# Third slot's weights in the second buffer, the inverse over two shares fewer, and one 64-column product for V and X from the ninth chunk

## The chip, the cores and the metric

The kernel runs on one core of one Trainium2 chip. A core has TensorE (PE in the rows, its weight loads apart as PEld), VectorE (DVE), ScalarE (ACT), GpSimd (POOL) and SyncE (SP, which here only issues transfers). The metric is the device time of one execution in microseconds, the median of three runs: 1097.17 us (1096.41 to 1097.25).

## The reference

Three parts follow one another. An attention recurrence over 4 batches x 8 heads (32 heads in all), 768 steps, head width 40, in float32:

```
y[t]  = r[t] @ state
Sa    = state @ a[t]
state = state * w[t] - outer(Sa, b[t]) + outer(v[t], k[t])
```

Its output, as 3072 tokens of 320 numbers, goes through a dense layer pair, `h = x @ w_in; x = max(0.01 h, h) @ w_out` (320 to 2048 to 320), and then through a mixture of eight experts of which each token uses one:

```
expert = argmax(x @ w_gate);  gate = softmax(x @ w_gate)[expert]
out    = gate * (relu(x @ w1[expert]) @ w2[expert])      # 320 -> 1024 -> 320
```

## The kernel before

**Attention in chunks.** The 768 steps are cut into 24 chunks of 32. Inside a chunk the recurrence becomes products of small matrices, one set for each head. Head n has its keys in tile `L` (three bands of rows, multiplied by state-side values in `Vx`), its queries in `Rr`, its values in `Vt`. A chunk goes through the steps `s1` to `s6`, most of them in halves a and b: `s1` forms right-hand sides, `s2` multiplies them by the inverse of a triangular matrix (`TT`) to get the corrected values X, `s3` forms the next state, `s3x` turns X around, `s4` multiplies queries by V and by X, `s5` makes the output, `s6` carries the state over. `s4` issues for each of 16 pairs of heads and each of V and X one product of a 40-row, 32-column weight with 32 columns of queries; in float32 each of them appears in the trace as two weight loads and two matmuls, 128 of each kind in a chunk (line 469). The V half of `Vt` comes by `load3` (line 384), the X half is written by ScalarE in `s3x` (line 459).

**Preparation and inverse.** Ahead of that, `prep` makes decays, keys and triangular matrices for a coming chunk, mostly on VectorE and GpSimd. For four chunks at a time GpSimd inverts the triangular matrices (`inverse`, lines 309 and 315, tile `Tinv`): 62 steps of one instruction each, of which VectorE does the first and the last, a transposition that leaves `TT` (line 323). From group to group this is needed by `s2` of chunks 8, 12, 16 and 20.

**The dense pair in halves.** Word `H` in the orders is half a step of the dense pair (`layer1` line 722, `layer2` line 738, with `g`, `gh`, `gl` between them on ScalarE, VectorE and GpSimd). The order of the whole first part is written out by hand as strings of words (`START`, `STEP`, `LATE`, `END`), played by `overlap`: one string a chunk from chunk 5 on. Word `w`, nine times in each such string, is a share of the inverse: it issues the remaining steps divided by the remaining shares, rounded up, so that the last share of a group of four chunks issues the last step.

**The experts in slots.** `Moe2.go` runs sixteen slots of 256 tokens, one expert each. In slot j TensorE does eight rounds f of `layer1` and `layer2` (lines 1152 and 1168); in the same rounds ScalarE and VectorE split the next slot's raw weights into two parts (`split`, lines 1114 to 1124), SP loads raw weights for the slot after (`load`, line 1072, five pieces of 512 or 640 KB), a gather fetches its tokens (`fetch`, lines 1086 to 1096: row numbers `sid` by SP, then rows `xg` by GpSimd), and TensorE turns the next slot's tokens (`xpose`, line 1135). Raw weights lie in `raw`; only slot 3 (`NE - 1`) uses a second tile, `raw2`. The load of slot 2 thus waits until the split of slot 1 has read `raw`, and it and the load of slot 3 behind it are issued piece by piece from round 1 of slot 0 on. Between them in SP's queue stand the row numbers of slot 2 and the last two writes of routed tokens (`x2d`, line 806), which wait for the gather of slot 2.

Of the kernel before, what the change touches and what calls it, by code (L numbers as in the profile page):

```python
# [73 lines left out]
def layouts(r, k, v, w, a, b, moe_w_in, moe_w_out, moe2_w_gate, moe2_w1, moe2_w2):  # L74
# [10 lines left out]

    def words(x):
        x = np.ascontiguousarray(x)
        return x.view(np.int64) if x.dtype == np.float64 else x
# [48 lines left out]
class Attn:  # L137


    def __init__(s, tc, ctx, i, k, xT, bad, psA):  # L140
        s.tc = tc
        nc = s.nc = tc.nc
# [16 lines left out]
        s.Vt = c.tile([128, 2, NU, 32], F32, name="Vt")  # L159
# [221 lines left out]
    def load3(s, c):  # L381
        nc = s.nc
        nc.sync.dma_start(s.Rr[64:104], s.i["hr"][c].rearrange("q (n d) -> q n d", d=32))
        nc.sync.dma_start(s.Vt[64:104, 0], s.i["hvt"][c].rearrange("q (n d) -> q n d", d=32))
        s.lamY = s.p1.tile([128, 16, 33], F32, name="lamY")
        nc.sync.dma_start(s.lamY.rearrange("p a b -> p (a b)"), s.dl[c])
# [631 lines left out]
class Moe2:  # L1018
# [36 lines left out]
    def source(s, j):  # L1055
        return s.raw2 if j == NE - 1 else s.raw
# [127 lines left out]
    def go(s, ready, finish):  # L1184
# [125 lines left out]
def overlap(tc, at, m1, plan):  # L1310
# [70 lines left out]
    def play(order, here=0):  # L1381
# [4 lines left out]
        for word in order:  # L1386
# [97 lines left out]
```

## Time and profile before

| | |
|---|---|
| median of three runs | 1097.17 us |
| the profiled execution, its own time | 1093.98 us |
| its span from first to last instruction | 1092.3 us |
[...]
| PE busy, weight loads busy | 926.7 us (85%), 870.0 us (80%) |
| DVE, ACT, POOL busy | 805.5, 529.9, 492.3 us |
| the chain that ended last, by engine | PE 41%, DVE 26%, DMA 12%, issue 8%, ACT 6%, POOL 5% |

All times in the rows are microseconds from the span's start. The chunks of the attention run until about 762, with the dense pair beside them; the rest of the dense pair ends at about 822, and the expert slots fill the remainder. A busy share says little alone: a wait is read from the bracket at the end of a timeline row, which says how long the engine stood idle before it and what released it. "Issue" as the releaser means that the profile shows nothing that the engine waited for. A window row gives busy time and, in brackets, the number of instructions of each engine that began in a stretch, then the granted clock.

### The profile page before, as it was taken

Reading aid. Unit: us, or ns where it says so; the run is one execution under the profiler, and the core shown is the slowest. Engines: PE = TensorE matmul, PEld = TensorE weight load, DVE = VectorE, ACT = ScalarE, POOL = GpSimd, SP = SyncE. Lnnn points to the kernel's source line nnn. Section 1 sums busy time; section 2 is a strip of 40 time slices with the busy share of each in tenths; the row PEclk is TensorE's granted clock in tenths of the full one; section 3 lists DMA queues with packets and bytes.
Section 4 is the critical chain, followed back from the end, with each engine's and each line's share of the span. In section 5 each row is a group of like instructions: output and inputs, shape, how many; then the busy total and the mean of one; then the engine's idle time right before and its main releaser. Section 6 shows DMA issues by size and latency. Waiting matters only on the chain.

```text
span 1092.3 us, 40673 instructions
## 1 busy us (share of the span) xinstructions
PE 926.7 (85%) x16854; PEld 870.0 (80%) x16854; DVE 805.5 (74%) x1910; ACT 529.9 (49%) x1316; POOL 492.3 (45%) x680
## 2 busy tenths in 40 slices
PE   2266677977799898989979998999999899999994
PEld 1255576867788887878879888998899799999994
DVE  8988778766878686968777766667657777787761
ACT  3545455653435444444435443444456556666651
POOL 5124135214883399446964685333553132332211
PEclk9999997788999899999999998999999999999997
DMA  8978876857546566574655542332425747444530
GB/s 249 228 211 228 231 198 185 214 137 215 137 126 172 143 166 158 129 176 131 172 151 146 128 80 72 92 82 54 152 91 129 219 158 225 126 146 140 161 104 17
DMA packets 143991, 166.04 MB, mean 152 GB/s; under 512 B 67931, under 2 KB 105451, under 8 KB 143671
## 3 DMA queue, kind: packets, MB, share of 16 engines
q1 hardware_dynamic: 133687, 144.20, 48.8%
q10 hardware_dynamic: 5760, 10.49, 3.3%
q0 software_dynamic: 4352, 8.69, 2.5%
q8 instruction: 134, 2.20, 0.9%
q14 instruction: 58, 0.48, 0.2%
HBM read 127.62 MB, written 42.27 MB: 156 GB/s over the span
## 4 chain that ended last, share of the span: by engine, by line
PE 41%; DVE 26%; DMA 12%; issue 8%; ACT 6%; POOL 5%; SPq 1%; POOLq 0%; DVEq 0%; ACTq 0%
PE psH L722 8%; PE psX L738 8%; PE epy L1168 8%; PE psH L1152 6%; DVE junk L762 4%; PE eph L1152 3%; DVE g L727 2%; DMA Pq<-Ms 2%; DVE Rr L472 2%; DMA L<-dKBr 2%; PE psA L414 2%; POOL Tinv L315 2%; DVE lam L226 2%; DMA raw<-hwe 1%; POOL itmp L309 1%
## 5 line engine op out<-in xcount | busy, mean ns | idle before, releaser
L729 POOL TENSOR_TENSOR gl<-g,gh 128x256 fp32r<-128x256 f32 x192 | 157.3, 822 | 216.9 <-ACT gh L728 199.6
L727 DVE TENSOR_TENSOR g<-psH,g 128x256 f32<-128x256 f32 x192 | 81.2, 423 | 103.3 <-ACT g L726 99.8
L728 ACT CAST gh<-g 128x256 fp32r<-128x256 f32 x192 | 77.9, 406 | 161.8 <-DVE g L727 159.6
L738 PE MATMUL psX<-woh,gh 128*128 128x320 f32 x384 | 134.6, 351 | 2.0 <-ACT woh L649 1.1
L738 PE MATMUL psX<-woh,gl 128*128 128x320 f32 x384 | 124.9, 325 | 4.2 <-POOL gl L729 4.0
L726 ACT ACTIVATE g<-psH 128x256 f32<-128x256 f32 x192 | 73.5, 383 | 108.6 <-PE psH L722 83.3
L738 PE MATMUL psX<-wol,gh 128*128 128x320 f32 x384 | 123.7, 322 | 0.0
L762 DVE SCALAR_TENSOR_TENSOR junk<-X,raws 128x320 bf16<-128x320 f32 x160 | 92.9, 581 | 5.5 <-ACT X L759 3.5
L722 PE MATMUL psH<-xh,wih 128*128 128x256 f32 x384 | 87.2, 311 | 3.6 <-DVE g L727 3.5
L309 POOL TENSOR_TENSOR itmp<-Tinv 128x30 f32<-128x30 f32 (+14 forms) x120 | 71.5, 596 | 33.5 <-DVE Tinv L301 26.3
L738 PEld LDWEIGHTS psX<-woh,gl 128*128 128x128 f32 x384 | 76.5, 199 | 7.6 <-POOL gl L729 7.3
L738 PEld LDWEIGHTS psX<-woh,gh 128*128 128x128 f32 x384 | 76.6, 199 | 6.2 <-ACT woh L649 1.3
L722 PE MATMUL psH<-xl,wih 128*128 128x256 f32 x384 | 80.6, 293 | 0.0
L722 PE MATMUL psH<-xh,wil 128*128 128x256 f32 x384 | 80.1, 291 | 0.0
L1180 POOL DMA_INDIRECT out<-ey,sid x32 | 32.5, 1015 | 104.6 <-ACT ey L1179 99.4
L265 PE MATMUL psA<-AtI,KB 40*64 40x72 f32 x1408 | 44.1, 266 | 41.7 <-DVE KB L243 18.4
L315 POOL TENSOR_TENSOR Tinv<-Tinv,itmp 128x30 f32<-128x30 f32 (+14 forms) x120 | 74.3, 619 | 7.8
L738 PEld LDWEIGHTS psX<-wol,gh 128*128 128x128 f32 x384 | 77.2, 201 | 0.4 <-DVE wol L650 0.3
L265 PEld LDWEIGHTS psA<-AtI,KB 40*64 40x64 f32 x1408 | 36.0, 164 | 48.8 <-POOL woh L242 18.4
L722 PEld LDWEIGHTS psH<-xh,wih 128*128 128x128 f32 x384 | 66.4, 201 | 8.6 <-DVE g L727 5.8
L722 PEld LDWEIGHTS psH<-xl,wih 128*128 128x128 f32 x384 | 63.2, 202 | 0.0
L1156 DVE SCALAR_TENSOR_TENSOR ehl<-psH,ehh 128x256 fp32r<-128x256 f32 x86 | 36.1, 420 | 36.4 <-ACT ehh L1155 36.1
(289 smaller groups left out, 2751.3 us busy)
## 6 DMA issues: line engine op xcount, KB each, us to landing
raw<-hwe SPq DMA_DIRECT2D x48, 512.0 KB
raw<-hwe SPq DMA_DIRECT2D x32, 640.0 KB
in<-h SPq DMA_DIRECT2D x23, 521.0 KB
KB<-h SPq DMA_DIRECT2D x22, 512.0 KB
L<-dKBr SPq DMA_DIRECT2D x24, 320.0 KB
dKBr<-KBr SPq DMA_DIRECT2D x22, 320.0 KB
lamY<-dl SPq DMA_DIRECT2D x24, 264.0 KB
dl<-lam SPq DMA_DIRECT2D x22, 264.0 KB
```

Of the source, the lines that this page charges most:

```text
L265: nc.tensor.matmul(box[i][64 * j:64 * j + 64, k, :], z["KB"][o, p, :], z["AtI"][o, p, :], start=True, stop=True)
L309: eng.tensor_tensor(out=box["v"], in0=T[:, k + 1:32, k:k + 1].to_broadcast([128, n, k]), in1=T[:, k:k + 1, 0:k].to_broadcast([128, n, k]), ...
L315: eng.tensor_tensor(out=T[:, k + 1:32, 0:k], in0=T[:, k + 1:32, 0:k], in1=box["v"], op=ALU.add)
L722: nc.tensor.matmul(ps[:, 0:256], w, x, start=(n == 0), stop=(n == 7))
L726: nc.scalar.activation(out=g, in_=ps[:, 0:256], func=AF.Copy, scale=0.01)
L727: nc.vector.tensor_tensor(out=g, in0=ps[:, 0:256], in1=g, op=ALU.max)
L728: nc.scalar.copy(out=gh, in_=g)
L729: return gh, gl, lambda: nc.gpsimd.tensor_tensor(out=gl, in0=g, in1=gh, op=ALU.subtract)
L738: nc.tensor.matmul(s.x2[t][:, 0:DM], x[:, o], w[:, f, :], start=(f == 0 and n == 0), stop=(f == NF - 1 and n == 2))
L762: nc.vector.scalar_tensor_tensor(out=s.junk, in0=X[:, t, 0:DM], scalar=1.0, in1=s.wg[:, e], op0=ALU.mult, op1=ALU.mult, accum_out=lg[:, t, ...
L1152: nc.tensor.matmul(ps, w, x, start=(n == 0), stop=(n == 7))
L1168: nc.tensor.matmul(s.y[t][:, 0:DM], x[:, o], w, start=(f == 0 and n == 0), stop=(f == 7 and n == 2))
```

## The change

There are three edits.

- `source`: slots 0, 1 and 3 use `raw`, slot 2 and all from slot 4 on use `raw2`. The five pieces of slot 2 are issued at once in round 0 of slot 0, those of slot 3 from round 5 of slot 0 on, behind the split of slot 1, which reads the same tile.
- `play`, word `w`: the remaining steps are divided by two shares fewer.
- From chunk 8 (`PAIRED`) on, V and X of a head lie side by side in `Vt`, 64 columns a head. The host lays out V with zeros where X goes, so `load3` moves 320 KB in place of 160 KB and writes the X places too; `s3x` writes X into every second block of 32; `s4` issues one product with a 64-column weight where it issued two.

```
--- before.py
+++ after.py
@@ -62,6 +62,7 @@
     "i H l t H H H H t l l H t l H H H l H s H H H H H H s H H H H H H s H H t H H H t H t H H c s s H H H H s H H l H H H H H H H H s H H H s x s H l H l H "
     "l s l H H "
 )
+PAIRED = 8
 NFIX = NT // SL + E // 2
 NTB = 8 * CAP + 8 * SL
 XW = DM + 64 + 1
@@ -82,6 +83,10 @@
 
     def flat(x):
         return np.ascontiguousarray(x.reshape(B, 2, 4, NC, C, D).transpose(3, 5, 1, 0, 2, 4).reshape(NC, D, NU * C))
+
+    def twice(x):
+        x = x.reshape(NC - PAIRED, D, NU, C)
+        return np.ascontiguousarray(np.concatenate([x, np.zeros_like(x)], axis=3).reshape(NC - PAIRED, D, 2 * NU * C))
 
     def words(x):
         x = np.ascontiguousarray(x)
@@ -101,7 +106,8 @@
         "nr": r, "nk": k, "nv": v, "nw": w, "na": a, "nb": b,
         "h1": np.ascontiguousarray(np.concatenate([hw, pad(pair(a)), pad(np.concatenate([pair(k), pair(b)], axis=-1))], axis=2)),
         "hr": flat(r),
-        "hvt": flat(v),
+        "hvt": np.ascontiguousarray(flat(v)[:PAIRED]),
+        "hvx": twice(flat(v)[PAIRED:]),
         "hv": np.ascontiguousarray(v.reshape(B, 2, 4, NC, C, D).transpose(3, 4, 1, 0, 2, 5).reshape(NC, C, NU * D)),
         "hwi": words(np.concatenate([moe_w_in[0:128], moe_w_in[128:256], np.concatenate([wt[:, 0:FF // 2], wt[:, FF // 2:]], axis=0)], axis=1)),
         "hwo": words(moe_w_out.reshape(NF, 128, DM).transpose(1, 0, 2).reshape(128, NF * DM)),
@@ -156,7 +162,7 @@
         s.L = [c.tile([128, NU, 40], F32, name=f"L{j}") for j in range(2)]
         nc.gpsimd.memset(s.Vx[1][32:64], 0.0)
         s.Rr = c.tile([128, NU, 32], F32, name="Rr")
-        s.Vt = c.tile([128, 2, NU, 32], F32, name="Vt")
+        s.Vt = c.tile([128, 2 * NU * 32], F32, name="Vt")
         s.Xq = c.tile([128, 512], F32, name="Xq")
         nc.vector.memset(s.Xq, 0.0)
         s.Pq = c.tile([128, 32, 32], F32, name="Pq")
@@ -381,7 +387,10 @@
     def load3(s, c):
         nc = s.nc
         nc.sync.dma_start(s.Rr[64:104], s.i["hr"][c].rearrange("q (n d) -> q n d", d=32))
-        nc.sync.dma_start(s.Vt[64:104, 0], s.i["hvt"][c].rearrange("q (n d) -> q n d", d=32))
+        if c < PAIRED:
+            nc.sync.dma_start(s.Vt[64:104, 0:32 * NU], s.i["hvt"][c])
+        else:
+            nc.sync.dma_start(s.Vt[64:104], s.i["hvx"][c - PAIRED])
         s.lamY = s.p1.tile([128, 16, 33], F32, name="lamY")
         nc.sync.dma_start(s.lamY.rearrange("p a b -> p (a b)"), s.dl[c])
 
@@ -451,7 +460,10 @@
 
     def s3x(s, c):
         nc = s.nc
-        vt = s.Vt[64:104, 1].rearrange("d (q g) t -> d g q t", q=4)
+        if c < PAIRED:
+            vt = s.Vt[64:104, 32 * NU:].rearrange("d (q g t) -> d g q t", q=4, t=32)
+        else:
+            vt = s.Vt[64:104].rearrange("d (n w t) -> d n w t", w=2, t=32)[:, :, 1].rearrange("d (q g) t -> d g q t", q=4)
         ps = s.bank()
         for g in range(4):
             nc.tensor.transpose(ps[:, 128 * g:128 * g + 128], s.Xq[:, 128 * g:128 * g + 128], s.k.ident)
@@ -464,9 +476,13 @@
         for p in range(8 * b, 8 * b + 8):
             for i in range(2):
                 n = 16 * i + p
+                if c >= PAIRED:
+                    nc.tensor.matmul(
+                        ps[64 * i:64 * i + 64, 32 * p:32 * p + 32], s.Vt[64:104, 64 * n:64 * n + 64], s.Rr[64:104, n, :], start=True, stop=True)
+                    continue
                 for w in range(2):
-                    o = 64 * i + 32 * w
-                    nc.tensor.matmul(ps[o:o + 32, 32 * p:32 * p + 32], s.Vt[64:104, w, n, :], s.Rr[64:104, n, :], start=True, stop=True)
+                    o, a = 64 * i + 32 * w, 32 * (NU * w + n)
+                    nc.tensor.matmul(ps[o:o + 32, 32 * p:32 * p + 32], s.Vt[64:104, a:a + 32], s.Rr[64:104, n, :], start=True, stop=True)
         o = slice(8 * b, 8 * b + 8)
         for i in range(2):
             nc.vector.tensor_tensor(
@@ -1053,7 +1069,7 @@
         s.nh = 0
 
     def source(s, j):
-        return s.raw2 if j == NE - 1 else s.raw
+        return s.raw if j < 2 or j == NE - 1 else s.raw2
 
     def load(s, j):
 
@@ -1206,10 +1222,13 @@
                 if sp and f % 3 != 2:
                     sp.pop(0)()
                 step(PACE[min(j, 2)][1])
-                if f == 1 and j + 2 < NFIX and j + 2 not in (NE - 1, NE):
+                if f == 0 and j == 0:
+                    for g in s.load(2):
+                        g()
+                if j == 0 and f == 5:
+                    ld = s.load(3)
+                if f == 1 and j + 2 < NFIX and j + 2 > NE:
                     ld = s.load(j + 2)
-                    if j + 2 == NE - 2:
-                        ld += s.load(NE - 1)
                 if f >= 1 and f != 3 and ld:
                     ld.pop(0)()
                 if f == 4 and j + 1 < NFIX:
@@ -1407,7 +1426,7 @@
                 if inv and not hurry:
                     inv.pop(0)()
             elif what == "w":
-                for _ in range(-(-len(inv) // (turns * (4 - here % 4) - k))):
+                for _ in range(-(-len(inv) // max(1, turns * (4 - here % 4) - k - 2))):
                     inv.pop(0)()
                 k += 1
             elif what == "L":
```

SP around the end of slot 0's first rounds, before: rows of `load` (raw, raw_14803 is the second tile), row numbers (sid) and routed tokens (x2d).

```order
L1072 DMA raw<-hwe 128x1024 [waits DMAHW4_49,DMAHW1_49,DVE_49]
L1083 TENSOR_LOAD ei
L1083 ISA x2
L1086 REGISTER_ALU
L1086 DMA sid_14887<-tbl_90 128x2 [waits DMAHW2_49,DMASW0_49]
L1086 REGISTER_ALU
L1086 DMA sid_14887<-tbl_91 128x2 [waits DMAHW3_49,DMASW1_49]
L1072 ISA
L1072 DMA raw<-hwe 128x1024 [waits DMAHW5_49,DVE_49]
L806 DMA x2d<-X_14770 4x32x385 [waits DMASW2_49,DMASW3_49,DVE_49,Activation_49]
L806 DMA x2d<-X_14770 4x32x385 [waits DMAHW6_49]
L1072 ISA
```

The same place after; raw_14291 is the second tile there.

```order
L1088 DMA raw_14291<-hwe 128x1024 [waits DMAHW3_49]
L1088 ISA
L1088 DMA raw_14291<-hwe 128x1280 [waits DMAHW4_49]
L1088 ISA
L1088 DMA raw_14291<-hwe 128x1280 [waits DMAHW5_49]
L1099 TENSOR_LOAD ei
L1099 ISA x2
L1102 REGISTER_ALU
L1102 DMA sid_14370<-tbl_90 128x2 [waits DMAHW6_49,DMASW0_49]
L1102 REGISTER_ALU
L1102 DMA sid_14370<-tbl_91 128x2 [waits DMAHW7_49,DMASW1_49]
L822 DMA x2d<-X_14258 4x32x385 [waits DMASW3_49,DMASW2_49,DMAHW0_49,DVE_49,Activation_49]
```

All five pieces of slot 2 now stand ahead of the row numbers and of the x2d writes, and wait for the end of the dense pair on PE alone; the pieces of slot 3 stand behind the writes, as before.

VectorE at the end of the first of the four inverses, before (Y is a chunk's output, il and KB a coming chunk's decays and keys, junk the routing logits).

```order
L493 TENSOR_TENSOR Y<-psA,lamY 40x512 [waits DMAHW5_49,DMAHW4_49,PE_49]
L493 TENSOR_TENSOR Y<-psA,lamY 40x512
L762 SCALAR_TENSOR_TENSOR junk,lg<-X_5293,raws 128x320 [waits DVE_49]
L239 SCALAR_TENSOR_TENSOR il<-in_4717,d1r 128x528
L727 TENSOR_TENSOR g<-psH,g 128x256 [waits Activation_49]
L762 SCALAR_TENSOR_TENSOR junk,lg<-X_5293,raws 128x320 [waits DVE_49]
L243 SCALAR_TENSOR_TENSOR KB<-KB,il 128x16x32 [waits DMAHW3_49,DVE_49]
L762 SCALAR_TENSOR_TENSOR junk,lg<-X_5293,raws 128x320 [waits DVE_49]
L727 TENSOR_TENSOR g<-psH,g 128x256 [waits Activation_49]
L762 SCALAR_TENSOR_TENSOR junk,lg<-X_5293,raws 128x320 [waits DVE_49]
L321 COPY Tinv<-one 128x32
L323 STREAM_TRANSPOSE TT<-Tinv 128x32x32 [waits DVE_49,Pool_49]
```

The same place after.

```order
L743 TENSOR_TENSOR g<-psH,g 128x256 [waits Activation_49]
L778 SCALAR_TENSOR_TENSOR junk,lg<-X_5300,raws 128x320 [waits DVE_49]
L327 COPY Tinv<-one 128x32
L329 STREAM_TRANSPOSE TT<-Tinv 128x32x32 [waits DVE_49,Pool_49]
L509 TENSOR_TENSOR Y<-psA,lamY 40x512 [waits DMAHW5_49,DMAHW4_49,PE_49]
L509 TENSOR_TENSOR Y<-psA,lamY 40x512
L778 SCALAR_TENSOR_TENSOR junk,lg<-X_5300,raws 128x320
L245 SCALAR_TENSOR_TENSOR il<-in_4724,d1r 128x528
L743 TENSOR_TENSOR g<-psH,g 128x256 [waits Activation_49]
L778 SCALAR_TENSOR_TENSOR junk,lg<-X_5300,raws 128x320 [waits DVE_49]
L249 SCALAR_TENSOR_TENSOR KB<-KB,il 128x16x32 [waits DMAHW3_49,DVE_49]
```

The transposition that leaves `TT` has moved ahead of the output and of the decay scan; the same holds at the other three inverses, and on GpSimd the last steps stand as much earlier.

PE at `s4` of chunk 8, before.

```order
L722 MATMUL psH<-xl,wis 128x256
L469 MATMUL psA<-Rr,Vt 32x32 [waits DMAHW2_49,DMAHW1_49,Activation_49]
L469 MATMUL psA<-Rr,Vt 32x32 x31
L469 MATMUL psA<-Rr,Vt 32x32 [waits Activation_49]
L469 MATMUL psA<-Rr,Vt 32x32 x31
L738 MATMUL psX_5366<-woh,gh 128x320
```

The same place after.

```order
L738 MATMUL psH<-xl,wis 128x256
L480 MATMUL psA<-Rr,Vt 64x32 [waits DMAHW2_49,DMAHW1_49,Activation_49]
L480 MATMUL psA<-Rr,Vt 64x32 x15
L480 MATMUL psA<-Rr,Vt 64x32 [waits Activation_49]
L480 MATMUL psA<-Rr,Vt 64x32 x15
L754 MATMUL psX_5375<-woh,gh 128x320
```

Two runs of 32 products have become two runs of 16; the waits are the same, and so it is in all sixteen chunks from 8 on.

## Rows read from the trace of the kernel before

**Rows 1.** The page's first part: busy time, share of the span, instructions of each engine.
```profile
PE 926.7 (85%) x16854; PEld 870.0 (80%) x16854; DVE 805.5 (74%) x1910; ACT 529.9 (49%) x1316; POOL 492.3 (45%) x680
```
**Rows 2.** Waits of line 469 over the whole run: releaser, us, times.
```profile
  issue: 38.4, 23
```
**Rows 3.** PE timeline around `s4`: start, us, operation, count, idle before.
```profile
371.19 0.32 PE L469 MATMUL psA<-Rr,Vt 40*32 40x32 f32 x5 [2.94 <-issue]
...
489.55 0.28 PE L469 MATMUL psA<-Rr,Vt 40*32 40x32 f32 x5 [4.64 <-issue]
...
709.68 1.32 PE L469 MATMUL psA<-Rr,Vt 40*32 40x32 f32 x128
...
712.00 1.64 PE L486 MATMUL psA<-Rr,L 104*40 104x32 f32 x64
```
**Rows 4.** Windows from one such stall to the next: engines' busy us (instructions), clock.
```profile
371.19:431.58 60.39, 54.41 (x1143) 50.28 (x1143) 47.91 (x115) 25.45 (x67) 48.96 (x68) 0.92 0.57 150
431.58:489.55 57.97, 50.65 (x1143) 47.27 (x1142) 44.50 (x113) 25.99 (x69) 28.93 (x38) 0.94 0.62 158
489.55:548.72 59.17, 53.34 (x1143) 49.10 (x1142) 45.79 (x110) 24.47 (x65) 46.63 (x65) 0.94 0.57 152
```
**Rows 5.** The page's DMA queues: instruction fetches, packets, MB, share of 16 engines.
```profile
q8 instruction: 134, 2.20, 0.9%
```
**Rows 6.** Windows, a chunk each (`s4` to `s4`): length, PE, PEld, DVE, ACT, POOL, clock.
```profile
313.45:341.30 27.85, 24.89 (x582) 22.90 (x581) 25.65 (x63) 12.46 (x33) 16.54 (x24) 1.00 0.56 149
...
366.48:397.68 31.20, 27.22 (x582) 25.34 (x581) 25.31 (x62) 12.77 (x33) 18.36 (x29) 0.89 0.59 155
397.68:427.43 29.75, 27.19 (x586) 25.03 (x586) 23.71 (x55) 13.25 (x35) 28.03 (x35) 0.94 0.62 162
427.43:458.66 31.23, 26.51 (x581) 24.47 (x580) 25.35 (x64) 12.67 (x33) 19.49 (x29) 0.95 0.52 136
...
484.07:516.18 32.11, 26.36 (x582) 24.29 (x581) 24.53 (x60) 12.78 (x33) 18.14 (x29) 0.89 0.54 147
...
545.94:577.24 31.30, 25.72 (x581) 23.07 (x580) 25.21 (x64) 12.51 (x33) 19.55 (x29) 1.00 0.52 137
...
654.61:685.43 30.82, 27.73 (x524) 25.76 (x523) 19.86 (x57) 9.98 (x27) 16.02 (x27) 0.83 0.27 75
685.43:709.68 24.25, 24.25 (x530) 22.64 (x529) 14.12 (x39) 12.24 (x31) 8.67 (x11) 1.00 0.38 91
```
**Rows 7.** Waits over the run, TensorE for `TT`: us, times, longest.
```profile
PE psA L414 <- DVE TT L323: 4.7, 3, 1.6
```
**Rows 8.** GpSimd timeline: the last step of the first inverse.
```profile
328.07 0.38 POOL L315 TENSOR_TENSOR Tinv<-Tinv,itmp 128x30 f32<-128x30 f32 x1
```
**Rows 9.** ScalarE and PE timelines in slot 1.
```profile
853.28 0.62 ACT L1118 CAST ah<-raw 128x512 fp32r<-128x512 f32 x1 [8.56 <-DMA raw<-hwe]
...
854.24 0.41 PE L1168 MATMUL epy<-bh,ehh 128*128 128x320 f32 x1 [3.79 <-ACT ehh L1155]
```
**Rows 10.** Windows of slot 1 and of slot 3 (columns as in rows 6, then GB/s).
```profile
839.44:861.50 22.06, 17.56 (x121) 16.82 (x121) 11.93 (x32) 9.61 (x20) 1.98 (x3) 0.92 0.88 226
876.50:891.80 15.30, 15.30 (x120) 15.30 (x119) 11.53 (x20) 9.76 (x20) 7.50 (x8) 1.00 0.42 144
```
**Rows 11.** SP timeline in slot 0: the x2d writes and the piece behind them.
```profile
837.86 1.23 SPq L806 DMA_DIRECT2D x2d<-X  x2
839.35 0.35 SPq L1072 DMA_DIRECT2D raw<-hwe  x1
```
**Rows 12.** The chain that ended last, in order of time: start, us, what.
```profile
839.95 15.68 DMA raw<-hwe
...
867.77 3.25 DMA xg<-x2d,sid
```
**Rows 13.** SP and ScalarE timelines at chunk 13: V's load, X's copy.
```profile
472.28 0.33 SPq L384 DMA_DIRECT2D Vt<-hvt  x1
...
479.47 0.58 ACT L459 COPY Vt<-psA 40x512 f32<-40x512 f32 x1
```

More of the change, by code (lines that the diff above doesn't have):

```diff
@@ L64 @@
 )
+PAIRED = 8
 NFIX = NT // SL + E // 2
@@ L383, in load3 @@
         nc.sync.dma_start(s.Rr[64:104], s.i["hr"][c].rearrange("q (n d) -> q n d", d=32))
[L384 removed]
+        if c < PAIRED:
+            nc.sync.dma_start(s.Vt[64:104, 0:32 * NU], s.i["hvt"][c])
+        else:
+            nc.sync.dma_start(s.Vt[64:104], s.i["hvx"][c - PAIRED])
         s.lamY = s.p1.tile([128, 16, 33], F32, name="lamY")
@@ L453, in s3x @@
         nc = s.nc
-        vt = s.Vt[64:104, 1].rearrange("d (q g) t -> d g q t", q=4)
+        if c < PAIRED:
+            vt = s.Vt[64:104, 32 * NU:].rearrange("d (q g t) -> d g q t", q=4, t=32)
+        else:
+            vt = s.Vt[64:104].rearrange("d (n w t) -> d n w t", w=2, t=32)[:, :, 1].rearrange("d (q g) t -> d g q t", q=4)
         ps = s.bank()
@@ L466, in s4 @@
                 n = 16 * i + p
+                if c >= PAIRED:
+                    nc.tensor.matmul(
+                        ps[64 * i:64 * i + 64, 32 * p:32 * p + 32], s.Vt[64:104, 64 * n:64 * n + 64], s.Rr[64:104, n, :], start=True, stop=True)
+                    continue
                 for w in range(2):
-                    o = 64 * i + 32 * w
-                    nc.tensor.matmul(ps[o:o + 32, 32 * p:32 * p + 32], s.Vt[64:104, w, n, :], s.Rr[64:104, n, :], start=True, stop=True)
+                    o, a = 64 * i + 32 * w, 32 * (NU * w + n)
+                    nc.tensor.matmul(ps[o:o + 32, 32 * p:32 * p + 32], s.Vt[64:104, a:a + 32], s.Rr[64:104, n, :], start=True, stop=True)
         o = slice(8 * b, 8 * b + 8)
@@ L1055, in source @@
     def source(s, j):
-        return s.raw2 if j == NE - 1 else s.raw
+        return s.raw if j < 2 or j == NE - 1 else s.raw2
     def load(s, j):
@@ L1208, in go @@
                 step(PACE[min(j, 2)][1])
-                if f == 1 and j + 2 < NFIX and j + 2 not in (NE - 1, NE):
+                if f == 0 and j == 0:
+                    for g in s.load(2):
+                        g()
+                if j == 0 and f == 5:
+                    ld = s.load(3)
+                if f == 1 and j + 2 < NFIX and j + 2 > NE:
                     ld = s.load(j + 2)
-                    if j + 2 == NE - 2:
-                        ld += s.load(NE - 1)
                 if f >= 1 and f != 3 and ld:
@@ L1409, in play @@
             elif what == "w":
-                for _ in range(-(-len(inv) // (turns * (4 - here % 4) - k))):
+                for _ in range(-(-len(inv) // max(1, turns * (4 - here % 4) - k - 2))):
                     inv.pop(0)()
```

8 lines of the change are left out of this document (6 added, 2 removed).

## The prediction

> **What bounds the kernel now.** I read the page's shares first, then the chain of waits, then windows of one chunk and one slot each, and last the timelines in the windows that are too long. TensorE is busy for 85% of the span [rows 1], and where nothing disturbs it a chunk or slot is TensorE's time exactly: 24.25 us of 24.25 in the chunk from 685.43 [rows 6], 15.30 of 15.30 in slot 3 [rows 10]. So the question is where TensorE stands still, and there are three kinds of such places, one for each edit.
>
> First, inside `s4`. There TensorE stops in the middle of a run of equal small products, with nothing that the profile shows to wait for: 2.94 us at 371, 4.64 us at 489 [rows 3]; over the run it is 38.4 us in 23 pieces [rows 2]. In the windows from one stall to the next the counts are 1143 matmuls each time [rows 4]: the stalls recur after the same number of instructions, and not after the same time (60.39, 57.97, 59.17 us). The instruction queue moved 2.20 MB in 134 packets [rows 5], while TensorE ran 16854 matmuls and as many loads [rows 1]: 33708 / 134 = 252 instructions a packet. 1143 + 1142 is 2285, plus some semaphore waits: nine packets. I read the stall as the wait for the next packet of instructions. `s4` is where it shows because it eats them fastest: 128 matmuls and 128 loads in 1.32 us [rows 3], a whole packet.
>
> Second, before `s2` of chunks 8, 12 and 16, where TensorE waits 4.7 us in three pieces for `TT` [rows 7].
>
> Third, slot 1: 22.06 us where slot 3 takes 15.30 [rows 10]. ScalarE waits 8.56 us for raw weights of slot 2, and TensorE 3.79 us for ScalarE [rows 9]; then the clock is at its lower level for a part (mean 0.92). The piece waited for stood behind the x2d writes on SP [rows 11] and took 15.68 us from there to landing [rows 12].
>
> **The 64-column product.** Removed are 64 matmuls and 64 loads a chunk, in 16 chunks. What the remaining ones take is not in the trace: the nearest row has the same count, 32 query columns and a 40-column weight in two column places, 1.64 us for 64 (line 486), against 1.32 us for the 128 of today [rows 3]. So the run itself costs between -0.6 (half of 1.32) and +0.3 us a chunk, -10 to +5 us in all; I take 0, near the row of line 486 less the overlap at its ends. What it may save is stalls. There are five from chunk 8 on: at 371 and 489 [rows 3], at the other two ends of the windows, 431.58 and 548.72 [rows 4], and one in the chunk from 654, whose clock is 0.83 [rows 6]. Price of a stall with its low clock, as window minus a like window without it [rows 6]: the chunks from 366 and 484 hold no wait for `TT`, so I compare with 27.85 (the chunk from 313) less its own 1.57 us of such a wait (4.7 / 3): 31.20 - 26.28 = 4.9 and 32.11 - 26.28 = 5.8. Those from 427 and 545 hold one as the reference does: 3.4 and 3.5. The chunk from 654 against 24.25: 6.6. Together 24 us.
>
> How many stay? A run of 256 instructions always contains the end of one packet, one of 128 in half the chunks; and a packet that holds such a run lasts longer, so that its successor has more time to come. On the other side two chunks shrink by exactly 256 instructions, from nine packets to eight: the packet ends again fall on the same places in every second chunk, and may fall into `s1`, `s2` or `s3`. I take two of the five stalls as left, or back elsewhere: 24 x 3/5 = -14. Bounds: -24 (none left) and 0 (five).
>
> [...]
>
> `load3` moves 160 KB more a chunk: at 162 to 75 GB/s, the rates in the last column of the windows [rows 6], 1.0 to 2.2 us of the queues, at most 35 us if all sixteen lay on the path. New is also that ScalarE's copy of X must wait for that load, with the dense pair's `g` and `gh` queued behind it. The load is issued 7.2 us ahead of the copy (472.28, 479.47) [rows 13], so doubling it stays covered. If the cover were gone the copy would be late by the excess alone. I take +1 us, for L and At behind it in SP's queue.
>
> **The inverse.** With two shares fewer the transposition that leaves `TT` stands some nine instructions earlier on VectorE. GpSimd's last step of today ends at 328.45 [rows 8], just in time, so the 4.7 us go (next late is the right-hand side of `s1`, already there), and the output `Y` and the decay scan come some 2 us later in their place. But the steps crowd: where a share has three steps GpSimd is full, 28.03 us of 29.75 in the chunk from 397, and there is the `gl` that layer 2 waits for. Some shares now have three steps where they had two; of these I count one or two steps of some 0.4 us (the last one takes 0.38 [rows 8]) into a full chunk: +0.7 us, four times. Net -4.7 + 2.7 = -2; bounds -5 and +3.
>
> **Slot 2's weights.** Slot 1's excess is 22.06 - 15.30 = 6.8 us [rows 10]; with the five pieces issued in slot 0 it goes. What is late next: the row numbers of slot 2 now stand behind all five pieces (2.8 MB) and not behind one; the gather, the x2d writes that wait for it, and the load of slot 3 behind those move too. Four pieces more at 226 GB/s [rows 10] are up to 10 us, less what the queue has free in slot 0, so the writes start at 838 to 848 in place of 837.86 [rows 11]. A piece behind them took 15.68 us [rows 12], so slot 3's first lands at 855 to 865; slot 2 asks for it at about 839.44 + 15.30 + 1 = 856. Late by 0 to 9. The gather of slot 3 is on the chain today already (867.77 to 871.02 [rows 12]), and the slot that needs it will begin 6.8 us sooner. So I keep 4.5 of the 6.8 us: -4.5; bounds -6.8 and +2.
>
> **Sum.** -14 + 1 - 2 - 4.5 = -19.5 us on the profiled execution's 1093.98 us, that is 1074.5. The median of the runs stands 3.2 us above that execution; I put the forecast on the median's side, 1097.2 - 19.5 = 1077.7, say 1078 us.
>
> **Rivals.**
>
> *As many stalls as before.* The fetch is late because its transfer is late, not because TensorE eats too fast; five stalls then sit elsewhere. For it: most chunks have the same runs and no stall (709 [rows 3]). Against it: the equal counts [rows 4]. 1097.2 - 2 - 4.5 + 1 = 1092.
>
> *No stall left.* `s4` never again empties a packet: 1097.2 - 24 - 2 - 4.5 + 1 = 1068. For it: all five sat in `s4`. Against it: 8 packets in two chunks keep their places, and `s1` to `s3` are bursts too.
>
> *The wait of slot 1 moves into slot 2*, on slot 3's pieces or its gather, and the crowded inverse eats the gain at `TT`: 1097.2 - 14 + 1 = 1084. For it: the 15.68 us behind the x2d writes.
>
> *Slower: packet ends locked into a burst.* With eight packets in two chunks a bad place repeats in all of them. One stall costs 24 / 5 = 4.8 us. The gain of the other edits is 5.5 us, so the kernel is slower by over 0.2% when more than 5 + (5.5 + 2.2) / 4.8 = 6.6 stalls remain, from seven on. With one in ten of the sixteen chunks: 1097.2 - 5.5 + 5 x 4.8 = 1116 us. For it: the period. Against it: any other burst takes fewer instructions in more time than `s4` (64 in 1.64 us).
>
> **How the numbers follow.** Forecast 0.45, no stall left 0.19, as many stalls 0.17, slot 2 0.12, slower 0.07. The forecast's own range is 1073 to 1083. For 8 in 10 I reach from 1066 (no stall left, and the product a little cheaper) to 1092 (as many stalls), which leaves out the slower case, half of the last microseconds of the first rival and a thin lower end. A measurement of this kernel tells 0.2%, 2.2 us, from no change. Faster than 1095: all cases but the slower one and some of the first rival, 0.88; within 0.2% 0.05; slower 0.07.
>
> **What would show it.** For the product: no or few idle rows "issue" on the line of `s4` after 341, chunk windows of 26 to 28 us in place of 31 to 32, counts of 1015 matmuls from one stall to the next if any are left; a run of 64 at about 1.3 to 1.6 us. For the inverse: no wait of line 414's successor for `TT`, and GpSimd's windows no longer than 30 us. For the slots: slot 1 at 15 to 16 us with ScalarE not waiting for raw weights; slot 2 at 15 to 18 us, and any excess with raw weights or `xg` as the releaser. It is wrong if the stalls move without getting fewer, if ScalarE waits for the load of V in `s3x`, or if `gl` waits pile up in the chunks from 397 and 516.

## The result, and the profile after

The changed kernel takes 1110.9 us (median of 5 runs, 1108.5 to 1111.8) against 1097.17 us before, slower by 13.7 us. The ratio is 1.0124; the brackets behind a ratio hold its 95% interval, here [1.0103, 1.0145]. The forecast was 1078 us; the range and the sign were both wrong.

The profiled execution took 1111.66 us, its span 1109.9 us, at a mean granted clock of 0.949 (1 is full speed). Its busy times first (columns as in [rows 1]), then its instruction queue (as in [rows 5]).

```profile
PE 941.0 (85%) x15830; PEld 884.4 (80%) x15830; DVE 800.7 (72%) x1910; ACT 530.0 (48%) x1316; POOL 492.9 (44%) x680
...
q8 instruction: 126, 2.06, 0.9%
```

A thousand matmuls fewer, and TensorE is busy for 14 us longer: 8.8 us of it are in the run of `s4` (below), and the mean clock is 0.949 where it was 0.954. The rest shows in waits of TensorE (us in all, times, longest): before, then after.

```profile
PE psA L469 <- issue: 16.0, 9, 4.6
...
PE psX L738 <- POOL gl L729: 4.0, 5, 1.2
```

```profile
PE psX L754 <- POOL gl L745: 17.6, 13, 2.7
...
PE epx L1151 <- DMA xg<-x2d,sid: 7.2, 2, 6.7
...
PE psA L480 <- issue: 0.5, 1, 0.5
```

**The stalls in `s4` are gone, and waits for `gl` stand in their place.** Of 16.0 us 0.5 are left. The 38.4 us of [rows 2] are not the measure: they add up what the matmuls (16.0) and what their weight loads (22.4) stood idle, mostly in the same stalls. From chunk 8 on TensorE still has eight idle pieces with nothing shown, of 0.3 to 0.9 us, four of them in `s3` (line 448); they sum to 4.2 us where before it was 16.3. But `layer2` waits 17.6 us for GpSimd's `gl`, which was 4.0. Windows after, chunks 10 and 11 (columns as in [rows 6]):

```profile
406.21:437.86 31.65, 28.89 (x523) 26.61 (x522) 22.09 (x54) 13.38 (x35) 29.55 (x40) 0.89 0.59 162
437.86:466.46 28.60, 25.80 (x518) 23.59 (x517) 25.27 (x63) 12.47 (x33) 14.35 (x20) 1.00 0.55 149
```

In chunk 10 GpSimd runs 40 instructions, busy for 29.55 us of 31.65; before it was 35 and 28.03 of 29.75 [rows 6]. What the queue looks like where TensorE waits, GpSimd first and then TensorE:

```profile
414.65 0.70 POOL L321 TENSOR_TENSOR Tinv<-Tinv,itmp 128x240 f32<-128x240 f32 x1
415.43 0.62 POOL L315 TENSOR_TENSOR itmp<-Tinv 128x238 f32<-128x238 f32 x1
416.13 1.56 POOL L321 TENSOR_TENSOR Tinv<-Tinv,itmp 128x238 f32<-128x238 f32 x1
417.66 1.23 POOL L745 TENSOR_TENSOR gl<-g,gh 128x256 fp32r<-128x256 f32 x1
```

```profile
418.94 0.42 PE L754 MATMUL psX<-woh,gl 128*128 128x320 f32 x1 [1.99 <-POOL gl L745]
```

Steps of the inverse stand ahead of the `gl` that TensorE needs. Behind this gap of 2 us the granted clock is at its lower level for a stretch, 0.50 in the window from 421 to 423 (the last three numbers are clock, DMA share and GB/s), and 0.89 on average in the chunk:

```profile
421.00:423.00 2.00, 2.00 (x70) 1.83 (x61) 0.00 (x0) 0.94 (x3) 1.76 (x4) 0.50 1.05 215
```

**Slot 1's wait moved into slot 2, and grew.** Slot 2 before, then slots 1 and 2 after:

```profile
861.50:877.20 15.70, 15.58 (x121) 15.30 (x120) 14.10 (x39) 9.85 (x20) 4.57 (x5) 1.00 0.59 200
```

```profile
851.43:866.82 15.39, 15.39 (x120) 15.38 (x120) 12.84 (x34) 9.31 (x20) 5.44 (x6) 1.00 0.60 70
866.82:894.64 27.82, 17.87 (x121) 17.07 (x120) 13.92 (x36) 10.07 (x21) 7.31 (x8) 0.88 0.67 243
```

Slot 1 is 6.7 us shorter [rows 10]; slot 2 takes 27.82 us where it took 15.70, so 5.5 us are lost in sum. The excess of slot 2 over a slot of 15.3 us is 12.5 us: 7.2 us of waiting for the gather of slot 3 (the row `xg` above), 2.7 us behind slot 3's raw weights (ScalarE waits 4.0 us for them, and TensorE for ScalarE), and 2.6 us in which TensorE is busy longer, at a mean clock of 0.88. The chain of waits through it:

```profile
855.15 13.00 DMA x2d<-X
...
868.27 10.14 DMA sid<-tbl
...
880.87 5.91 DMA xg<-x2d,sid
...
886.83 1.33 PE epx L1151 x5
```

SP's queue in that time, and GpSimd's timeline where the row numbers of slot 2 and of slot 3 have come:

```profile
833.41 7.40 SPq L1088 DMA_DIRECT2D raw<-hwe  x7
841.65 0.89 SPq L1102 DMA_DIRECT2D sid<-tbl  x2
855.15 1.23 SPq L822 DMA_DIRECT2D x2d<-X  x2
859.10 5.04 SPq L1088 DMA_DIRECT2D raw<-hwe  x5
865.01 14.12 SPq L1102 DMA_DIRECT2D sid<-tbl  x4
```

```profile
849.23 0.19 POOL L1109 TENSOR_TENSOR sid<-sid 128x2 int32<-128x2 int32 x1 [15.85 <-DMA sid<-tbl]
...
878.64 0.19 POOL L1109 TENSOR_TENSOR sid<-sid 128x2 int32<-128x2 int32 x1 [20.24 <-DMA sid<-tbl]
```

The latter in the kernel before:

```profile
865.44 0.23 POOL L1093 TENSOR_TENSOR sid<-sid 128x2 int32<-128x2 int32 x1 [19.08 <-DMA sid<-tbl]
```

The row numbers of slot 2 go out behind all pieces, at 841.65, and land at 849.23. Their gather follows, and only then, at 855.15, the x2d writes. Slot 1 as a whole begins 12.0 us later in this trace than in the one before, so the times are to be read from its start: the writes go out 3.7 us behind it, where they went 1.6 us ahead of it [rows 11], 5.3 us later. Behind them stand the pieces of slot 3 and then the row numbers of slot 3, whose landing takes 10.14 us. These come 27.2 us behind the start of slot 1 and came 26.0 us behind it before, hardly later; but their gather lands 5.91 us after its issue where it took 3.25 [rows 12], so that it ends 3.8 us later (35.4 and 31.6 us behind the start of slot 1), and TensorE asks for it 3.5 us sooner (27.7 and 31.2). These two make up the 7.2 us.

**The run of `s4` is longer.** Groups of instructions, TensorE's matmuls of `s4`: before, then after (64 columns from chunk 8 on, 32 in the first eight).

```profile
L469 PE MATMUL psA<-Rr,Vt 40*32 40x32 f32 x3072 | 39.3, 203 | 25.1 <-issue 16.0 <-DMA Vt<-hvt 4.3 <-ACT Vt L459 2.5
```

```profile
L480 PE MATMUL psA<-Rr,Vt 40*64 40x32 f32 x1024 | 33.3, 220 | 0.5 <-issue 0.5
L485 PE MATMUL psA<-Rr,Vt 40*32 40x32 f32 x1024 | 14.8, 212 | 9.2 <-DVE wt_t L604 4.5 <-ACT Vt L471 2.3 <-ACT KBr L277 2.1
```

In sixteen chunks it is busy for 33.3 us where it was 39.3 - 14.8 = 24.5: 0.55 us more a chunk, with half the instructions.

### The profile page after: what moved, and what is told of

The parts are those of the page before. It is cut to its first block, busy times and chain, and to the rows that moved or that the text cites. A ratio compares the mean times of both kernels' runs of the same rounds, so it can differ in the third digit from the quotient of the medians.

```text
span 1109.9 us, 38636 instructions
## 1 busy us (share of the span) xinstructions
PE 941.0 (85%) x15830; PEld 884.4 (80%) x15830; DVE 800.7 (72%) x1910; ACT 530.0 (48%) x1316; POOL 492.9 (44%) x680
## 3 DMA queue, kind: packets, MB, share of 16 engines
q8 instruction: 126, 2.06, 0.9%
## 4 chain that ended last, share of the span: by engine, by line
PE 46%; DVE 18%; DMA 11%; POOL 9%; issue 9%; ACT 5%; SPq 0%; POOLq 0%; DVEq 0%; ACTq 0%
PE psH L738 9%; PE psX L754 8%; PE epy L1184 8%; PE psH L1168 6%; DMA x2d<-X 4%; POOL Tinv L321 3%; PE eph L1168 3%; POOL itmp L315 3%; PE psA L423 3%; POOL gl L745 2%; DVE g L743 2%; DMA Pq<-Ms 2%; PE psA L480 2%; PE psA L448 2%; PE psA L502 1%
## 5 line engine op out<-in xcount | busy, mean ns | idle before, releaser
L754 PE MATMUL psX<-woh,gl 128*128 128x320 f32 x384 | 125.2, 326 | 17.6 <-POOL gl L745 17.6
L754 PEld LDWEIGHTS psX<-woh,gl 128*128 128x128 f32 x384 | 76.3, 199 | 22.4 <-POOL gl L745 21.3
L315 POOL TENSOR_TENSOR itmp<-Tinv 128x30 f32<-128x30 f32 (+14 forms) x120 | 68.2, 568 | 30.4 <-DVE Tinv L307 22.6
L738 PEld LDWEIGHTS psH<-xh,wil 128*128 128x128 f32 x384 | 63.7, 204 | 0.0
```

The costliest lines, as they stand in the source:

```text
L315: eng.tensor_tensor(out=box["v"], in0=T[:, k + 1:32, k:k + 1].to_broadcast([128, n, k]), in1=T[:, k:k + 1, 0:k].to_broadcast([128, n, k]), ...
L738: nc.tensor.matmul(ps[:, 0:256], w, x, start=(n == 0), stop=(n == 7))
L754: nc.tensor.matmul(s.x2[t][:, 0:DM], x[:, o], w[:, f, :], start=(f == 0 and n == 0), stop=(f == NF - 1 and n == 2))
```

## The experiments

Each ratio is to runs of the kernel before on the same chip; their median lay between 1088.2 and 1097.2 us from chip to chip, so ratios are compared and not times. Differences in us are between medians on one chip; a ratio can come out up to 2 us from them.

**The three edits, each alone.** The theory: slots and inverse cost, the product gains.

*Edit 1, the slots* (`source` and the two places of `load` in the diff).

> Before with the first edit alone (slot 2's raw weights to the second tile). Theory: it gives what the changed kernel's trace shows, slot 1 at 15.4 us in place of 22.1 (-6.7) and slot 2 at 27.8 in place of 15.7 (+12.1), because the row numbers of slot 2, then the x2d writes, then the row numbers of slot 3 stand behind one another on SP: about +5 us, 1102. Rival: the long slot 2 comes of the later clock and order that the other edits leave, and alone the edit gains its 6.7 us: 1090.

Measured: 1102.0 us, 1.0052 [1.0027, 1.0077], 4.9 us slower, as the theory had it. Slots 1 and 2 take 15.46 and 28.05 us, and the x2d writes go out 4.0 us behind the start of slot 1: the whole effect is there without the other edits.

*Edit 2, the inverse* (the one line of word `w`).

> Before with the second edit alone (the inverse over two shares fewer). Theory: GpSimd is the bound of the chunks in which the inverse runs, and one step more in a share makes layer 2 wait for gl: chunks 5 to 7 grew by 5.6 us together in the changed kernel, and four groups give +15 to +25 us, 1112 to 1122, with waits of line 738 for gl. Rival (as predicted): the wait for TT goes and the crowding costs less, -2 to +3 us.

Measured: 1112.0 us, 1.0121 [1.0086, 1.0156], 14.9 us slower. TensorE's waits for `gl` and for nothing shown in `s4`:

```profile
PE psA L469 <- issue: 14.2, 7, 3.7
PE psX L738 <- POOL gl L729: 10.7, 8, 3.1
```

The wait for the inverse's `TT` [rows 7] is gone, the one for `gl` is 6.7 us longer. By itself that row is weak evidence: in edit 1's run, whose first part is that of the kernel before, it says 8.3 us. And it is not the whole price. In this trace (20.7 us longer than the one before) all waits of TensorE together grew by 7.4 us, and the same 16854 matmuls kept it busy for 13.7 us longer [rows 1], at a mean clock of 0.942 where it was 0.954:

```profile
PE 940.4 (84%) x16854; PEld 882.8 (79%) x16854; DVE 802.2 (72%) x1910; ACT 530.9 (48%) x1316; POOL 492.0 (44%) x680
```

*Edit 3, the product* (`Vt`, `load3`, `s3x`, `s4`).

> Before with the third edit alone (V and X side by side, one 64-column product from chunk 8 on). Theory: the five stalls inside s4 go (-24 us), and each chunk's s4 takes 1.84 us in place of 1.12 to 1.45 (some +0.6 us, 16 times, +10): about -14 us, 1083. Rival: the product and the doubled load cost more than the stalls give back, and the whole loss of the changed kernel is here: 1105 to 1110.

Measured: 1096.4 us, 0.9987 [0.9962, 1.0013], no change; both expectations missed. Windows of chunks 9, 11, 13, 15 and 19:

```profile
371.30:399.68 28.38, 26.10 (x518) 23.57 (x517) 24.56 (x60) 12.45 (x33) 18.02 (x29) 1.00 0.71 178
...
429.42:461.26 31.84, 28.54 (x517) 26.19 (x516) 25.46 (x64) 12.46 (x33) 19.46 (x29) 0.89 0.53 140
487.46:515.91 28.45, 27.00 (x517) 24.85 (x516) 24.35 (x60) 12.55 (x33) 18.01 (x29) 0.94 0.65 168
545.69:577.48 31.79, 27.27 (x517) 24.85 (x516) 25.71 (x64) 12.52 (x33) 19.48 (x29) 0.95 0.53 141
655.36:683.67 28.31, 26.56 (x459) 24.55 (x459) 20.90 (x57) 9.99 (x27) 16.25 (x27) 0.94 0.32 85
```

```profile
PE psX L754 <- POOL gl L745: 9.0, 9, 1.6
...
PE psA L480 <- issue: 1.0, 3, 0.4
```

No stall is left in `s4`, but against [rows 6] only three of the five chunks are shorter, by 2.8, 3.7 and 2.5 us; chunks 11 and 15 are 0.6 and 0.5 us longer. Net 7.9 us, of which the other chunks from 8 on, where only the run is longer, take back about half. One trace against one is a rough measure: chunk 6, which edit 3 leaves as it was, is 2.9 us longer in this one. The 9.0 us for `gl` are hardly above the 8.3 of edit 1's run.

**The row numbers ahead of the pieces.** Edit 1, and in round 0 of slot 0:

```
+ s.fetch(2); third = s.fetch(3, later=True)   # row numbers of slots 2 and 3; steps of slot 3's gather in slot 1
  for g in s.load(2): g()
```

> The first edit, with the row numbers of slots 2 and 3 issued ahead of slot 2's five pieces (slot 3's gather stays where it was). Theory: the wait of slot 2 came of these row numbers standing behind the weights and the x2d writes: slot 1 at 15.4 us, slot 2 at 15.4 to 20 (slot 3's pieces still stand behind the x2d writes), 1090 to 1095. Rival: slot 2 waits for slot 3's weights behind the x2d writes, whatever the row numbers do: slot 2 at 24 us or more, no gain over the first edit alone.

Measured: 1089.4 us, 0.9925 [0.99, 0.9951], 7.7 us faster than before where edit 1 alone was 4.9 slower. Slots 1 and 2 are as the theory had them:

```profile
846.03:861.43 15.40, 15.40 (x121) 15.39 (x120) 13.13 (x36) 9.75 (x20) 1.97 (x3) 1.00 0.80 131
861.43:876.79 15.36, 15.36 (x120) 15.35 (x119) 13.15 (x34) 9.54 (x20) 6.56 (x8) 1.00 0.77 280
```

SP's queue has the writes 1.0 us ahead of the start of slot 1, 4.7 us earlier in the slot than after the change:

```profile
845.06 1.23 SPq L806 DMA_DIRECT2D x2d<-X  x2
```

The edit moves two things at once, the row numbers of slot 2 (and with them its gather, the writes and slot 3's weights) and those of slot 3; which of them gives how much was not run apart.

**The paired layout with two products.** Edit 3, but in `s4`

```
+ for w in range(2): ... s.Vt[64:104, 64 * n + 32 * w:64 * n + 32 * w + 32] ...
```

> Only the layout of edit 3: V and X side by side from the ninth chunk, load3 with its 320 KB, the same copy of X, but two products of 32 columns per head as before. Theory (what edit 3 costs is the 64-column run itself, 1.84 us for 64 against 1.1 to 1.45 us for 128, and what it gives is the stalls; load and copy are covered): the run of 128 takes 1.1 to 1.45 us again, the stalls with nothing to wait for are back in s4 (12 to 17 us over the run, against 1.0 with the 64-column product), and the time is that of before, 1095 to 1099 us. Rival (the doubled load on SP's queue or the strided copy is what eats the gain of edit 3): slower than before by 5 to 12 us, 1102 to 1109 us, with waits for Vt or for L and At behind it.

Measured: 1.0021 [0.9998, 1.0044], no clear difference. The run of 128 takes 1.34 us again (at 603.61), and the stalls are back, in the five chunks of the prediction and at the same products of the run: 5, 29, 53, 76 and 7 of them are left behind the stall, as in the kernel before (the row at 489.55 in [rows 3] says 5 only because its window ends there).

```profile
PE psA L481 <- issue: 16.5, 5, 4.7
```

So load and copy cost 2.3 us or nothing (at most 4.8 by the interval), and it is the 64-column product that ends the stalls. It has half the instructions and spreads them over a longer run; these runs do not tell the one from the other. That a stall is a wait for instructions fits its fixed places, but no row shows the fetch itself.

**`gl` off GpSimd.** `layer1` gives its `gl` to VectorE in some strings of the order; `n` is 1 here (strings two and three of each group of four) and 0 in a later run:

```
- lambda: nc.gpsimd.tensor_tensor(out=gl, ...)
+ lambda: s.small.tensor_tensor(out=gl, ...)   # in play: VectorE if 4 < here < 20 and here % 4 > n
```

The trace counts 64 of them, not 70 as expected; one takes 0.56 to 0.59 us there, 0.82 on GpSimd. With edit 2, without it, and with edit 3:

> Edit 2 alone, and in the second and third string of each group of four (from chunk 6 to chunk 19) the low half gl is made by VectorE and not by GpSimd, 70 of 192 of them. Theory (edit 2 alone was slower by 15 us since shares of four steps in place of three stand ahead of gl in a GpSimd queue that is full): gl no longer stands behind the steps, TensorE's waits for it fall from 10.7 us to under 4, and the time comes back to 1092 to 1100 us. Rival (the transposition that leaves TT, now ahead of the output and the decay scan on VectorE, is what delays): 1108 to 1114 us, no better than edit 2 alone. A third case, VectorE full with 70 more operations of some 0.4 us (3.5 us a chunk beside 24 to 25 us of 30): waits for g, RH and Rr grow and the time is above 1100 us.

> The kernel before with the same 70 gl on VectorE and nothing else. Theory (GpSimd is full only beside the inverse): waits for gl (4.0 us) and for the inverse's TT (4.7 us) shrink, VectorE has the room; 1089 to 1096 us. Rival (VectorE becomes the bound of these chunks): 1100 to 1108 us. Beside edit 2 with the same, the difference of the two is what edit 2 costs without the crowding: -5 to 0 by the theory, +10 to +15 by its rival.

> Edit 3 alone with the same 70 gl on VectorE. Theory (the five stalls that edit 3 removed were in part replaced by waits for gl, 4.0 to 9.0 us, since the same GpSimd steps must now run in shorter chunks): with these gone edit 3 gives 5 to 9 us over the kernel with gl alone, 1083 to 1090 us. Rival (the stalls were worth no more than what the longer runs cost, 0.6 us in sixteen chunks): as the kernel with gl alone, within 3 us.

Measured: 1.0053 [1.0031, 1.0075], 1.0002 [0.9981, 1.0023] and 0.9975 [0.9955, 0.9995]. Edit 2's price falls from 14.9 to 6 us, where the theory wanted about nothing: 4.8 us of waits for GpSimd's `gl` were left, in the first strings. Edit 3 gives 4.0 us over its control (2.9 by the ratios, whose intervals overlap), between theory and rival. The windows of chunks 11 and 15, with `gl` moved: with the old product, and with the paired one.

```profile
429.72:457.80 28.08, 25.85 (x581) 24.20 (x580) 25.81 (x69) 12.47 (x33) 10.54 (x17) 0.94 0.55 147
545.41:573.39 27.98, 24.96 (x582) 22.97 (x581) 25.73 (x68) 12.37 (x33) 10.42 (x17) 1.00 0.56 151
```

```profile
426.94:454.87 27.93, 25.53 (x517) 23.67 (x516) 25.69 (x68) 12.39 (x33) 10.46 (x17) 1.00 0.58 154
540.87:568.95 28.08, 25.66 (x517) 23.70 (x516) 25.80 (x69) 12.39 (x33) 10.61 (x17) 1.00 0.59 155
```

The 3 us by which these two were too long [rows 6] go with GpSimd's work (19.5 to 10.5 us busy), whichever product `s4` uses; with edit 3 alone they stayed, at 31.84 and 31.79 us, though no stall was left. They were not the stall's.

**All strings, and the repairs together.**

> Edit 2 alone with gl on VectorE in the first string of each group too (96 of 192 gl). With strings two and three alone edit 2 still cost 5.8 us, and TensorE's waits for GpSimd's gl that were left (4.8 us in 3 pieces) sat at gl of first strings, behind shares of four steps. Theory (edit 2 costs by gl behind the steps of the inverse, and by nothing else): no gl stands behind a step, waits for gl by GpSimd under 1.5 us, the ratio to before falls to 0.997 to 1.002. Rival (half of its price is the place of the VectorE work or the longer VectorE load): the ratio stays at 1.004 to 1.008. A third case, VectorE too full with 32 more of 0.58 us: above 1.008.

> The whole change with two repairs: the row numbers of slots 2 and 3 ahead of the five pieces, and gl on VectorE in strings one to three. Theory (what made the change slower is these two waits): from 1.0124 to 0.986 to 0.994, faster than before, waits for gl by GpSimd under 2 us where the change had 17.6, slot 2 at 15.4 us where it had 27.8. Rival (edit 2 has a price of its own that no place of gl takes away): 0.995 to 1.002.

Measured: 1.0072 [1.0046, 1.0098] and 0.9992 [0.9972, 1.0013]; both on the rivals' side. But chunks 8, 12 and 16, which hold no inverse, had become longer. They are here with the repaired change, then without edit 2 and with `gl` in strings two and three alone:

```profile
342.68:370.30 27.62, 25.75 (x523) 24.04 (x522) 19.99 (x55) 12.78 (x34) 7.81 (x8) 1.00 0.72 178
459.54:489.83 30.29, 28.84 (x522) 26.89 (x522) 20.10 (x55) 12.97 (x34) 7.81 (x8) 0.89 0.72 167
579.01:609.29 30.28, 28.82 (x522) 26.92 (x522) 20.10 (x55) 12.96 (x34) 7.81 (x8) 0.89 0.63 151
```

```profile
344.19:370.11 25.92, 25.41 (x523) 23.88 (x522) 18.89 (x51) 12.77 (x34) 11.14 (x12) 1.00 0.71 174
459.61:485.59 25.98, 25.57 (x522) 23.90 (x521) 18.89 (x51) 12.77 (x34) 11.14 (x12) 1.00 0.72 177
574.73:600.87 26.14, 25.71 (x522) 23.93 (x521) 18.88 (x51) 12.78 (x34) 11.15 (x12) 1.00 0.70 169
```

That is 10 us of the experiment's own making, and these two runs say nothing on edit 2. The same with `gl` of the first string moved only from `s5` on, where the inverse begins: edit 2 (e13 in the texts below), its control without edit 2 (e14), and the repaired change.

> Edit 2 alone, gl on VectorE in strings two and three of a group and in string one from s5 on, where the inverse's steps begin (76 rows of gl). Theory (edit 2 costs only through gl behind steps of GpSimd; the 11 us in chunks 8, 12 and 16 of the run with all of string one came from VectorE's gl ahead of s2): these chunks are back at 25 to 26 us each, waits for gl on GpSimd stay under 1.5 us, and the time is within 2 us of the same kernel without edit 2 (e14). Rival (edit 2 has a price of its own, by the transposition and the lag of the rest of GpSimd's work): 5 us or more over e14.

> The control: the kernel before with the same gl on VectorE, without edit 2. Theory: as the kernel with strings two and three on VectorE, ratio 0.998 to 1.003. If the added gl cost by themselves, 1.003 or more, and e13 is read against that.

> The whole change, the row numbers of slots 2 and 3 first, and gl as in e13. Theory: as the kernel without edit 2 (ratio 0.9891), 0.987 to 0.992. Rival (edit 2 has its own price): 0.994 to 0.999.

Measured: 1.0026 [1.0, 1.0051], 1.0011 [0.9983, 1.0038], 0.9921 [0.9892, 0.9951]; the last lies at the edge of its theory, and its interval reaches into the rival's range. Chunks 8, 12 and 16 are back at 26.0 to 26.3 us in it, so `gl` on VectorE ahead of `s2` was what made them longer. Edit 2 is now 1.7 us over its control, within the noise, and TensorE's wait for GpSimd's `gl` with it is down to one row, the same as in the control:

```profile
PE psX L739 <- POOL gl L730: 0.3, 1, 0.3
```

So its price goes when `gl` leaves GpSimd. Moving `gl` also takes 0.8 us of work a piece off GpSimd, so the runs do not tell its place behind the steps from the length of the queue. Edit 2 has no gain either: of the 4.7 us at `TT` 2.9 are left in the control, and taking them away bought nothing that these runs can tell.

**What is left when one or two repairs are made.**

> The whole change with one repair, the row numbers of slots 2 and 3 ahead of the five pieces; gl on GpSimd as ever. Theory (the slots and the chunks add): the change's ratio 1.0124 falls by what the same repair gave edit 1 alone, 1.0052 to 0.9925 or 12.7 thousandths, to 0.998 to 1.002; waits for gl stay at 12 to 20 us. Rival (a later tail hid part of the wait): 1.004 or more.

> The same without edit 3. Theory: gl alone measured 1.0002, so the ratio is that of the slots with the row numbers first, 0.990 to 0.995, and the kernel with edit 3 beside it is 3 to 5 us faster. Rival: the two within 2 us of each other.

> Edit 1 with the row numbers of slots 2 and 3 ahead of the five pieces, edit 3, and gl on VectorE in strings two and three; the inverse as before. Theory (the parts lie in different stretches and add): 0.9925 for the slots times 0.9975 for the paired product with gl, a ratio of 0.988 to 0.992. Rival (edit 3 gives nothing beside a tail that is no longer late): 0.992 to 0.995.

Measured: the change with the row numbers first 1.0020 [0.9998, 1.0041], with 19.0 us of waits for `gl` (slots 15.40 and 15.35 us); slots, row numbers and `gl`, without the product, 0.9941 [0.9921, 0.9962]; and with the product 0.9891 [0.987, 0.9912], 1082.0 us where the kernel before took 1093.7. All three are as their theories had them. The last is the fastest of all, 11.7 us better than before; it leaves edit 2 out. The product is worth 4.6 us here, and the two intervals lie apart: this is the clear sign that it gains, once GpSimd is not late behind it.

## Why the prediction was wrong

The edits alone measured +4.9, +14.9 and -0.8 us; the prediction had -4.5, -2 and -13. Their sum is 19.0 us, and together they took 13.7; with intervals of 3 to 4 us on each the two are not clearly different.

**Bound: right.** TensorE was the bound, and its idle places were those named. What failed is what stood behind each.

**Inverse: the failed step with most weight.** "Some shares now have three steps where they had two; of these I count one or two steps ... into a full chunk: +0.7 us, four times." In GpSimd's instruction order the stretches of steps between two `gl` at a group's begin are 2, 6, 3, 3, 12 long before and 3, 8, 4, 4, 12 after: shares of three became shares of four, and five steps more stand ahead of the same `gl`. The price of 0.4 us a step was wrong too: it was taken from the last step, the narrowest (30 elements), while the mean is 0.57 to 0.62 us. Five steps of 0.6 us are 3 us a group and 12 us in four, by estimate; 14.9 were measured, with the 4.7 us at `TT` already gained. The rest is not accounted for singly; in edit 2's trace most of the loss shows as the same matmuls taking longer at a lower mean clock. That `gl` on GpSimd is where the price arises is shown, since it goes when `gl` leaves GpSimd (1.7 us over the control). The prediction saw the right queue and named these waits as what would make it wrong; it took the number of steps from an impression of the windows and not from the order, where it could be counted.

**Slots: the failed step is a term put at nothing.** Slot 1 lost its 6.8 us as forecast. "Late by 0 to 9 ... I keep 4.5 of the 6.8 us" priced the weights of slot 3 behind the writes, and that part held: the writes moved by 5.3 us from the start of slot 1, inside the 0 to 10 (845.76 in edit 1's own trace, with 838 to 848 forecast), and the weights cost TensorE 2.7 us. What got no price is the gather of slot 3, though the prediction had it on the chain and said that the slot that needs it begins sooner. It cost 7.2 us, and the lower clock behind the waits 2.6. The excess of slot 2 was 12.5 us and the net effect +4.9, outside the bounds of -6.8 and +2. The run with the row numbers first gives the whole 6.8 us, and 0.9 more.

**Product: fewer stalls than forecast, and no gain by itself.** Forecast were two of five stalls left or back elsewhere; none was in `s4` (0.5 us), with pieces of at most 0.9 us elsewhere. How many would stay was worked out from some 252 instructions a packet, the author's estimate. The changed kernel moved 8 packets fewer (134 and 126) for 2048 instructions of TensorE fewer (1024 matmuls and as many loads), 256 each by these counts; that a stall stands at the end of a packet was not shown. The reading of [rows 2] as 38.4 us was wrong (16.0 for the matmuls), but no price hung on it. The price of 24 us failed. It came from windows of unlike chunks: chunk 7 was the measure for chunks whose GpSimd and VectorE work differs. Without a stall chunks 9, 13 and 19 take 28.3 to 28.5 us, not 26.3 or 24.25; chunks 11 and 15 were held by GpSimd. "So the run itself costs between -0.6 (half of 1.32) and +0.3 us a chunk, ... I take 0": it was 0.55 by the busy times, outside the bounds, 8.8 us in sixteen chunks. The row of line 486 that it leaned on had the same counts, but a 64-wide weight takes 2.06 us for 64 (at 693.94 after) and not 1.64. That waits for `gl` also grow because TensorE stalls less and comes sooner to them (9.0 us with edit 3 alone) is a likely reading and not shown.

**`load3`: right.** Taken at +1; the run with the paired layout and two products, which has all of it, measured 2.3 us by its ratio [-0.2, 4.8].

**What the stalls cost.** The stalls of `s4` came back with the two products (16.5 us in 5 pieces, the longest 4.7). What they cost in time is not shown by itself, since the product that ends them has the longer run: net it gave 0.8 us alone, 4.0 and 4.6 us with `gl` moved.

**Rivals.** "No stall left" came true for the stalls of `s4`, and not for their price. The wait that moves into slot 2 came true as well, nearly twice as large: an excess of 12.5 us in slot 2, where the rival let it take back the 6.8. The one with packet ends locked into a burst did not: no stall of `s4` is left that could repeat.

## What to carry to other kernels

A stall is worth what the next engine lets the time fall (here ending most of 16.0 us of stalls gave a net 0.8 us, and 4.0 to 4.6 us with `gl` moved), so price it by a window of the same chunk without it, or by the next late engine in that window, and not by its length. Compare places in two traces from the start of the same stretch, since everything ahead of it shifts them: 12 of the 17 us by which the x2d writes were late had nothing to do with the slots. Where an edit moves work within an engine's queue, count in the instruction order what stands ahead of each consumer, before and after: five steps of 0.6 us a group account for most of the price here, by estimate. And when a large load is issued early, issue ahead of it the small transfers (row numbers, 128 x 2) that others hang on: with that, 4.9 us slower became 7.7 us faster.

## What the hardware showed unexpectedly

- A 40 x 64 weight with 32 columns takes 2.06 us for 64, and twice as many of 40 x 32 take 1.32: fewer instructions, more time.
- The five stalls of `s4` stand at the same products of the run in the kernel before and in the run with the paired layout and two products.
- A transfer of 128 x 2 numbers took 10.14 us behind the x2d writes and five pieces of weights.
- Two like steps of the inverse on GpSimd (128 x 240 and 128 x 238 elements) took 0.70 us at 414.65 and 1.56 us at 416.13.
- `gl` takes 0.82 us on GpSimd and 0.56 to 0.59 us on VectorE, and still VectorE is the worse place for it ahead of `s2` (10 us in three chunks).
